# A copy of C taken from SBUF, per-tile first loads and a re-costed planner in a chunked-attention and MLP chain

## The chip, the core and the metric

The kernel runs on one core of one Trainium2 chip. The metric is the device time of one execution in microseconds. Engines are named as in the profile: PE is TensorE, DVE is VectorE, ACT is ScalarE, POOL is GpSimd, SP is SyncE, whose queue issues every DMA here.

## The reference

The inputs are x (4 x 8 x 768 x 32: batch, head, position, width), a (4 x 8 x 768), B and C (4 x 8 x 768 x 16), and four weights. First comes a decaying linear attention, by chunks; then two MLPs on 3072 tokens of width 256 with a hidden width of 2048.

```python
cum = np.cumsum(la, axis=-1)                              # la = log(a) in the chunk
L = np.exp(cum[..., :, None] - cum[..., None, :]) * causal
y[:, :, sl] = einsum('bhij,bhjd->bhid', (Cc @ Bc.T) * L, xc) \
            + einsum('bhin,bhnd->bhid', Cc, state) * np.exp(cum)[..., None]
state = exp(sum(la)) * state + sum_j(Bc x xc * exp(cum[-1] - cum))
...
h = x @ w_in;  g = elu(h);                     x = g @ w_out      # layer 1
h = x @ w_in2; g = h * tanh(softplus(h));      out = g @ w_out2   # layer 2
```

## The kernel before, in words

A chunk has T = 96 positions, so there are 8 chunks; chunk c of batch b is tile i = 4c + b, and the 32 tiles are numbered from 0. The four tiles of a chunk make one block of 384 tokens for the MLPs. The blocks' MLP work is cut into slots (`order`, `at_slot`, L685 to L692): a slot is one group of 128 hidden columns of one layer for one block, so there are 16 slots of layer 1 and 16 of layer 2 for each block, 256 in all. A slot is `emit_h` (L694, six matmuls), the activation on ACT and DVE, from slot 16 on a split of its result into a high and a low part (`split_hi`, `split_lo`, L735 and L741), and `emit_y1` or `emit_y2` (L750, L785). The weights come in 32 jobs of 512 KB (`load_job`, L258) and pass through five steps, `job_1` to `job_5` (L279 to L322), on DVE, ACT and either ACT, DVE or POOL.

A tile of attention loads x (`load_x`, L236), C and B (`load_bc`, L224, and for the four tiles of the first chunk `load_bc0`, L215) and a row of the decays, broadcast over 96 partitions (`at_cumrow`, L453, out of a DRAM copy that `cum_4`, L390, writes). `at_diff`, `at_mask` and `at_exp` make the decay matrix L. For tiles 0 to 2 (`TR0`, L44) C and B are transposed on PE (`at_tr0`, L555), copied out (`at_tr0_out`, L564), and the scores are made in fp32 (`at_scores0`, L587; `at_p0`, L596, multiplies by L). For the other tiles `three_parts` (L893) splits C and B into three bf16 parts: `at_split_1` and `at_split_3` (L459, L470) on ACT, `at_split_2` and `at_split_4` (L465, L476), each of two subtractions, on DVE or POOL, and `at_split_5` (L482), a DMA transpose; `at_scores` and `at_p` follow (L602, L610). From the second chunk on, C is needed a second time, on partitions 96 to 127, three rows of 32 positions beside each other: `load_bc` brings it with three more DMAs from DRAM (L231 to L233). `at_cs` (L523, POOL) scales it, `at_rc` and `at_rc2` (L541, L550) transpose and copy it into the matrix that `at_y` (L627) multiplies by x and the state. `at_y_hi` and `at_y_lo` (L642, L649) take the result out of PSUM as the two parts on which layer 1 works. The transposes, scores and, after the first chunk, the results of a tile share one PSUM buffer, `s`.

The order of all this is set by a planner inside the kernel. Each `step` (L71) names an engine or a choice of engines with a cost in us, a function that issues its instructions, and the steps it depends on. `Ring` (L83) stands for a set of buffers: `take` gives the user of a buffer the list of steps that must be done before it. `run_steps` (L102) first works out for each step how late it may start, then runs a list scheduling with one clock for each engine; SP has a second clock, `moved`, at which the DMA engines are through with what was issued, so a DMA step has the cost of its issue, the time that its data takes, and a landing (L191 to L196). At the end the functions are called in the order of the planned starts, and that is the order of each engine's queue. On the chip each engine takes its queue strictly in order and waits where an input is not there. A cost in the planner therefore never delays anything by itself; it decides what stands in front of what, and on which engine.

```python
late[k] = min([dl] + [late[q] - lat(...) for q in succ[k]]) - sum(...)   # L123
...
k, o, r, cost = min((c for c in can if c[2] <= t + 0.02), key=lambda c: (urgency(c[0], e), c[0]))   # L183
```

Of the kernel before, what the change touches and what calls it, by code (L numbers as in the profile page):

```python
# [17 lines left out]
def tile_chain(  # L18
# [25 lines left out]
    TR0 = (0, 1, 2)  # L44
# [38 lines left out]
    class Ring:  # L83
# [18 lines left out]
    def run_steps():  # L102
# [5 lines left out]
        deps = [sorted(set(flat(e[1]))) for e in steps]  # L108
        succ = [[] for _ in range(n)]
        for k, ds in enumerate(deps):  # L110
            for d in ds:
                succ[d].append(k)
# [6 lines left out]
        while todo:  # L119
# [3 lines left out]
            late[k] = min([dl] + [late[q] - lat(opts[0][0], steps[q][0][0][0]) for q in succ[k]]) - sum(  # L123
                opts[0][3:4], opts[0][1]
            )
            for d in deps[k]:
# [5 lines left out]
        left = [len(deps[k]) for k in range(n)]  # L132
        done = {}
# [12 lines left out]
        def ready(k, e):  # L146
            return max([0.0] + [done[d][1] + lat(done[d][0], e) for d in deps[k]])
# [16 lines left out]
        for _ in range(n):  # L164
            best = None
            for e, ks in open_.items():
                can = []
                for k, o, r, cost in ks:
                    opts = steps[k][0]
                    if len(opts) > 1:  # L170
# [15 lines left out]
            t = max(t, r)  # L186
            free[e] = t + loads(k, e) + cost
# [14 lines left out]
        for _, k, o in sorted(order):  # L202
            steps[k][0][o][2]()
# [11 lines left out]
    def load_bc0(src, d, tag):  # L215

        t = tp.tile([T, NB, H, N], F32, tag=tag, name="bc0")
        nc.sync.dma_start(
            out=t.rearrange("p b h n -> p (b h) n"), in_=src[:, :, 0:T, :].rearrange("b h s n -> s (b h) n")
        )  # L220
        for i in range(NB):
            d[i] = t[:, i]

    def load_bc(i):  # L224
# [600 lines left out]
    s_lc = step((DQ, 0.48, lambda: load_bc0(Cm, c_t, "xyh"), 1.34))  # L825
    s_lb = step((DQ, 0.48, lambda: load_bc0(Bm, b_t, "xyl"), 1.34))
# [7 lines left out]
    s_q4 = [step((DQ, 0.62, lambda c=c: cum_4(c), 0.07), s_q3) for c in range(NCH)]  # L834
# [26 lines left out]
    w_ready = {}  # L861
    r_1, _ = take("raw")
    r_2, _ = take("raw")
    for j, (key, k) in enumerate(jobs):
        rf, rn = take("raw") if j >= NJ else ([], [])
        q0 = step((DQ, 0.48, lambda j=j: load_job(j), 1.46), rn)
        q1 = step((V, 0.42, lambda j=j: job_1(j)), q0)
# [25 lines left out]
    def three_parts(i, need):  # L893
# [23 lines left out]
    for i in range(NB):  # L917
        cold = i in TR0
        if cold:
            tf, tn = take("s")  # L920
            tr = step((PE, 0.64, lambda i=i: at_tr0(i)), s_lc, s_lb, s_c2, tn)
# [4 lines left out]
        else:  # L926
            a2, a5, tf = three_parts(i, [s_lc, s_lb])
# [10 lines left out]
        else:  # L938
# [30 lines left out]
        y = step((PE, 0.95, lambda i=i: at_y(i)), pz, LX[i], an)  # L969
# [5 lines left out]
        bw = step((G, 0.36, lambda i=i: at_bw_1(i)), s_lb, s_d3, bn)  # L975
# [14 lines left out]
    for i in range(NB, tiles):  # L990
        c, b = divmod(i, NB)
        bcf, bcn = take("bc")
        lb = step((DQ, 2.38, lambda i=i: load_bc(i), 0.4), bcn)
# [4 lines left out]
        for g in range(2):  # L998
            f = lambda e, i=i, g=g: at_diff(i, g * H // 2, (g + 1) * H // 2, e)
            dd.append(step(alt(f, (G, 0.79), (V, 0.47)), lc, s_q6))  # L1000
        mk = step((G, 0.85, lambda i=i: at_mask(i)), dd)
        ex = step((A, 0.73, lambda i=i: at_exp(i)), mk)
        table[ex] = "exp"
        cs = step((G, 0.79, lambda i=i: at_cs(i)), lb, lc, s_d5)
        r_f, r_n = take("r")
        rc = step((V, 0.47, lambda i=i: at_rc(i)), cs, r_n)
        rc2 = step(alt(lambda e, i=i: at_rc2(i, e), (V, 0.27), (A, 0.41)), rc)
        bcf += [a2, cs]
        if c + 1 < NCH:
            bf, bn = take("bw")  # L1010
            b1 = step((G, 0.36, lambda i=i: at_bw_1(i)), lb, s_d3, bn)
# [116 lines left out]
```

## Time and profile before

| | us |
|---|---|
| median of the runs shown (3 runs) | 660.62 |
| lowest and highest | 657.75, 661.45 |
| the profiled execution, its own time | 658.91 |
| its span, first to last instruction | 657.2 |
| mean granted clock of PE in it | 0.974 of full speed |

A row of the timeline gives the start, the duration, the engine, the line, the operation, its output and input and how many instructions were merged into it; in brackets stands how long the engine was idle just before, and what ended that. A row by line gives busy us, the mean of one in ns, then idle time in front. A row of waits reads "who waited <- for whom: us in total, times, longest". A DMA row gives KB of each and the median us from issue to landing.

### The profile page before, as it was taken

To read this page: it belongs to the slowest core of one execution; us is meant where nothing else is said; L and a number is where in the kernel's file an instruction comes from. 1 tells how busy PE (TensorE), PEld (TensorE's weight loads), DVE (VectorE), ACT (ScalarE), POOL (GpSimd) and SP (SyncE) were. 2 spreads that over 40 slices of the span, in tenths; PEclk is the share of its full clock that TensorE was granted. 3 is DMA by queue.
4 is the path that set the end of the run, shared out by engine and by line. 5 is a ranking of instruction groups with operands and counts; after the bars stand their busy time and mean duration, and the time that the engine had idled before them with its cause. 6 is when DMAs were issued, how large, how long until landed. Compare 5 with 4: busy or idle time off the path is not lost.

```text
span 657.2 us, 12318 instructions
## 1 busy us (share of the span) xinstructions
PE 613.4 (93%) x4488; PEld 583.4 (89%) x4488; DVE 490.0 (75%) x1018; ACT 370.1 (56%) x704; POOL 190.4 (29%) x220
## 2 busy tenths in 40 slices
PE   4578898999999999999899999999999989999996
PEld 4466668999989989998899989999999989999996
DVE  5699999997579899647975689758985586654443
ACT  4576758696367656445855477445865464442221
POOL 3478584301054484005410244003410040000000
PEclk9569998999999999999999999999999999999999
DMA  8897875331355473015530264105430120000000
GB/s 149 181 280 175 190 150 141 118 113 49 73 91 92 81 117 58 1 10 101 88 58 1 50 99 83 26 0 104 88 58 0 43 43 17 9 1 1 9 18 24
DMA packets 160221, 49.14 MB, mean 75 GB/s; under 512 B 145920, under 2 KB 148992, under 8 KB 160160
## 3 DMA queue, kind: packets, MB, share of 16 engines
q1 hardware_dynamic: 160160, 48.36, 35.5%
q8 instruction: 35, 0.57, 0.4%
q14 instruction: 26, 0.21, 0.1%
HBM read 33.69 MB, written 3.24 MB: 56 GB/s over the span
## 4 chain that ended last, share of the span: by engine, by line
PE 65%; DVE 16%; DMA 10%; issue 3%; SPq 2%; ACT 1%; POOL 1%; DVEq 0%; POOLq 0%; ACTq 0%
PE h L702 10%; PE h L703 10%; PE h L704 10%; DMA d<-cum_d 6%; PE acc L793 6%; PE acc L764 5%; PE acc L765 5%; PE acc L766 5%; PE acc L795 5%; PE acc L794 5%; DVE raw L298 2%; DMA raw<-in_moe_w_in_dram 2%; DMA t<-stk 2%; DVE r L612 2%; DVE gl L744 1%
## 5 line engine op out<-in xcount | busy, mean ns | idle before, releaser
L702 PE MATMUL h<-xyh,wi 128*128 128x384 f32 x512 | 177.6, 347 | 3.0 <-ACT xyh L647 2.9
L703 PE MATMUL h<-xyl,wi 128*128 128x384 f32 x512 | 173.1, 338 | 1.3 <-DVE xyl L653 1.3
L704 PE MATMUL h<-xyh,wi 128*128 128x384 f32 x512 | 172.7, 337 | 0.0
L744 DVE TENSOR_TENSOR gl<-w,gh 128x384 fp32r<-128x384 f32 x221 | 135.8, 614 | 20.4 <-ACT gh L306 8.6
L748 ACT ACTIVATE w<-h 128x384 f32<-128x384 f32 x128 | 61.8, 490 | 106.6 <-PE h L704 104.4
L793 PE MATMUL acc<-wo,gh 128*128 128x256 f32 x384 | 112.7, 293 | 0.2 <-DVE xyl L780 0.2
L795 PE MATMUL acc<-wo,gl 128*128 128x256 f32 x384 | 108.2, 282 | 0.0
L794 PE MATMUL acc<-wo,gh 128*128 128x256 f32 x384 | 108.1, 282 | 0.0
L702 PEld LDWEIGHTS h<-xyh,wi 128*128 128x128 f32 x512 | 97.6, 191 | 5.7 <-ACT xyh L647 3.2
L703 PEld LDWEIGHTS h<-xyl,wi 128*128 128x128 f32 x512 | 97.5, 191 | 2.5 <-DVE xyl L653 2.0
L308 DVE CAST gh<-w 128x384 fp32r<-128x384 f32 x135 | 53.2, 394 | 60.3 <-PE acc L794 38.9
L704 PEld LDWEIGHTS h<-xyh,wi 128*128 128x128 f32 x512 | 97.1, 190 | 0.0
L717 ACT ACTIVATE w<-h 128x384 f32<-128x384 f32 x112 | 54.5, 488 | 49.8 <-PE h L704 49.5
L764 PE MATMUL acc<-gh,wo 128*128 128x384 f32 x224 | 75.6, 338 | 2.7 <-DVE xyl L780 2.7
L766 PE MATMUL acc<-gl,wo 128*128 128x384 f32 x224 | 75.4, 337 | 0.0
L765 PE MATMUL acc<-gh,wo 128*128 128x384 f32 x224 | 75.4, 337 | 0.0
L793 PEld LDWEIGHTS acc<-wo,gh 128*128 128x128 f32 x384 | 72.5, 189 | 2.1 <-DVE xyl L780 0.5
L795 PEld LDWEIGHTS acc<-wo,gl 128*128 128x128 f32 x384 | 72.8, 190 | 0.0
L794 PEld LDWEIGHTS acc<-wo,gh 128*128 128x128 f32 x384 | 72.6, 189 | 0.0
L306 ACT ACTIVATE gh<-w 128x384 fp32r<-128x384 f32 x105 | 55.0, 524 | 29.2 <-PE acc L765 21.6
L725 DVE TENSOR_SCALAR w<-w 128x384 f32<-128x384 f32 x99 | 40.5, 410 | 30.2 <-ACT w L717 29.9
L493 POOL TENSOR_TENSOR d<-d,dk 96x384 f32<-96x384 f32 x35 | 37.4, 1075 | 83.1 <-DMA d<-cum_d 80.2
(103 smaller groups left out, 951.5 us busy)
## 6 DMA issues: line engine op xcount, KB each, us to landing
d<-cum_d SPq DMA_DIRECT2D x31, 288.0 KB, 3.6
raw<-in_moe_w_in_dram SPq DMA_DIRECT2D x16, 512.0 KB, 4.2
raw<-in_moe_w_out_dram SPq DMA_DIRECT2D x16, 512.0 KB, 4.4
xs<-in_x_dram SPq DMA_DIRECT2D x32, 96.0 KB, 3.3
out_dram<-o SPq DMA_DIRECT2D x16, 96.0 KB, 1.9
bc<-in_C_dram SPq DMA_DIRECT2D x28, 48.0 KB, 2.3
bc<-in_B_dram SPq DMA_DIRECT2D x28, 48.0 KB, 2.7
bc<-in_C_dram SPq DMA_DIRECT2D x84, 16.0 KB, 2.1
```

The source lines that it names most:

```text
L306: nc.scalar.activation(out=out, in_=in_, func=AF.Copy)
L702: nc.tensor.matmul(out=h, lhsT=hi[:, k, fs], rhs=xh[:, k, :], start=(k == 0), stop=False)
L703: nc.tensor.matmul(out=h, lhsT=hi[:, k, fs], rhs=xl[:, k, :], start=False, stop=False)
L704: nc.tensor.matmul(out=h, lhsT=lo[:, k, fs], rhs=xh[:, k, :], start=False, stop=(k == 1))
L744: alu(eng).tensor_tensor(out=gl, in0=w, in1=gh.bitcast(F32), op=ALU.subtract)
L748: nc.scalar.activation(out=new_w(s), in_=st[s][0], func=AF.Mish)
L764: nc.tensor.matmul(out=y, lhsT=hi[:, f % FP, ds], rhs=gh, start=(f == 0), stop=False)
L765: nc.tensor.matmul(out=y, lhsT=lo[:, f % FP, ds], rhs=gh, start=False, stop=False)
L766: nc.tensor.matmul(out=y, lhsT=hi[:, f % FP, ds], rhs=gl, start=False, stop=(f == NF - 1))
L793: nc.tensor.matmul(out=y, lhsT=gh[:, ts], rhs=hi[:, f % FP, :], start=(f == 0), stop=False)
L794: nc.tensor.matmul(out=y, lhsT=gh[:, ts], rhs=lo[:, f % FP, :], start=False, stop=False)
L795: nc.tensor.matmul(out=y, lhsT=gl[:, ts], rhs=hi[:, f % FP, :], start=False, stop=(f == NF - 1))
```

## The change

It does five things. `load_bc0` brings one tile of C or B per call, so the first block is loaded by eight DMAs into the same two buffers. `TR0` takes in tile 3, which so goes the way of tiles 0 to 2. The three loads of C for partitions 96 to 127 move out of `load_bc` into a step of their own, `load_c96`, which copies from the tile of C already in SBUF and depends on its landing. The planner gets three rules: the first users of a ring's buffers start in the order of the ring (`Need`, `after`), the steps of a list in `in_turn` start in the order of that list, and POOL's steps and the DVE steps in `lock` are never planned at the same time (`held`). And many costs are changed. Steps that start at the same planned time are now issued in the order in which they were planned. The work is otherwise the same; which engine takes a step that has a choice can differ. Of the diff some cost lines and repeats are left out.

```diff
-    TR0 = (0, 1, 2)
+    TR0 = (0, 1, 2, 3)
...
+    lock = set()
+    in_turn = []
...
-            return self.free[k], (self.free[k - self.n] if k >= self.n else [])
+            return self.free[k], Need(self, k, self.free[k - self.n] if k >= self.n else [])
+    class Need:
+        def __init__(self, ring, k, free):
+            self.ring, self.k, self.free = ring, k, free
...
+        after = [[] for _ in range(n)]
+        for ks in in_turn:
+            for p, q in zip(ks, ks[1:]):
+                after[q].append(p)
+        for users in first.values():
+            ks = [users[q] for q in sorted(users)]
+            for p, q in zip(ks, ks[1:]):
+                if p != q and p not in deps[q]:
+                    after[q].append(p)
         succ = [[] for _ in range(n)]
         for k, ds in enumerate(deps):
-            for d in ds:
+            for d in ds + after[k]:
                 succ[d].append(k)
...
+            late[k] = min([late[k]] + [late[q] for q in succ[k] if k not in deps[q]])
...
-            return max([0.0] + [done[d][1] + lat(done[d][0], e) for d in deps[k]])
+            return max([0.0] + [done[d][1] + lat(done[d][0], e) for d in deps[k]] + [begun[d] for d in after[k]])
...
+                    if e == V and k in lock:
+                        r = max(r, held[G])
+                    elif e == G:
+                        r = max(r, held[V])
...
+            begun[k] = t
+            if e == G or e == V and k in lock:
+                held[e] = t + cost
...
-        for _, k, o in sorted(order):
+        place = {k: i for i, (_, k, _) in enumerate(order)}
+        for _, _, k, o in sorted((t, place[k], k, o) for t, k, o in order):
...
-    def load_bc0(src, d, tag):
-        t = tp.tile([T, NB, H, N], F32, tag=tag, name="bc0")
-        nc.sync.dma_start(
-            out=t.rearrange("p b h n -> p (b h) n"), in_=src[:, :, 0:T, :].rearrange("b h s n -> s (b h) n")
-        )
-        for i in range(NB):
-            d[i] = t[:, i]
+    def load_bc0(src, d, tag, i):
+        if i == 0:
+            tl[tag] = tp.tile([T, NB, H, N], F32, tag=tag, name="bc0")
+        d[i] = tl[tag][:, i]
+        nc.sync.dma_start(out=d[i], in_=src[i, :, 0:T, :].rearrange("h s n -> s h n"))
     def load_bc(i):
...
         sl = slice(c * T, (c + 1) * T)
         nc.sync.dma_start(out=t[0:T, 0], in_=Cm[b, :, sl, :].rearrange("h s n -> s h n"))
         nc.sync.dma_start(out=t[0:T, 1], in_=Bm[b, :, sl, :].rearrange("h s n -> s h n"))
+        c_t[i], b_t[i], c96_t[i] = t[0:T, 0], t[0:T, 1], t[T:128]
+    def load_c96(i):
         for k in range(3):
-            sl = slice(c * T + 32 * k, c * T + 32 * k + 32)
-            nc.sync.dma_start(out=t[T:128, k], in_=Cm[b, :, sl, :].rearrange("h s n -> s h n"))
-        c_t[i], b_t[i], c96_t[i] = t[0:T, 0], t[0:T, 1], t[T:128]
+            nc.sync.dma_start(out=c96_t[i][:, k], in_=c_t[i][32 * k:32 * k + 32])
...
-    s_lc = step((DQ, 0.48, lambda: load_bc0(Cm, c_t, "xyh"), 1.34))
-    s_lb = step((DQ, 0.48, lambda: load_bc0(Bm, b_t, "xyl"), 1.34))
+    s_lc = [step((DQ, 0.48, lambda i=i: load_bc0(Cm, c_t, "xyh", i), 0.95)) for i in range(NB)]
+    s_lb = [step((DQ, 0.48, lambda i=i: load_bc0(Bm, b_t, "xyl", i), 0.95)) for i in range(NB)]
...
-    s_q4 = [step((DQ, 0.62, lambda c=c: cum_4(c), 0.07), s_q3) for c in range(NCH)]
+    s_q4 = [step((DQ, 0.62, lambda c=c: cum_4(c), 0.2), s_q3) for c in range(NCH)]
...
-        q1 = step((V, 0.42, lambda j=j: job_1(j)), q0)
+        q1 = step((V, 0.36, lambda j=j: job_1(j)), q0)
+        lock.add(q1)
...
+        lock.add(q3)
+        q4 = step(alt(lambda e, j=j: job_4(j, e), (A, 0.58), (V, 0.34)), q3)
+        q5 = step(alt(lambda e, j=j: job_5(j, e), (G, 1.33), (V, 0.60)), q4,
                   dl=slot_time(2 * NF + k * FP) + 10.0 if j >= NJ else 1e9)
+        lock.update((q4, q5))
...
-        LX[i] = step((DQ, 0.48, lambda i=i: load_x(i), 0.55), n)
+        LX[i] = step((DQ, 0.48, lambda i=i: load_x(i), 0.95), n)
+    in_turn.append([s_la])
+    for i in range(NB):
+        in_turn[-1] += [s_lc[i], s_lb[i], LX[i]] + LW[i:i + 1]
...
-        a2 = step(alt(lambda e: at_split_2(i, e), (V, 0.40), (G, 0.78)), a1, rn)
+        a2 = step(alt(lambda e: at_split_2(i, e), (V, 0.40), (G, 0.45)), a1, rn)
         a3 = step((A, 0.62, lambda: at_split_3(i)), a2)
-        a4 = step(alt(lambda e: at_split_4(i, e), (V, 0.40), (G, 0.78)), a3)
+        a4 = step(alt(lambda e: at_split_4(i, e), (V, 0.40), (G, 0.45)), a3)
         tf, tn = take("t")
-        a5 = step((DQ, 0.62, lambda: at_split_5(i), 1.34, True), a4, tn)
+        a5 = step((DQ, 0.62, lambda: at_split_5(i), 2.0, True), a4, tn)
+        lock.update((a2, a4))
...
-            sc = step((PE, 0.33 if cold else 0.24, lambda z=z: at_scores(i, z)), a5, pn)
+            sc = step((PE, 0.4 if cold else 0.33, lambda z=z: at_scores(i, z)), a5, pn)
...
-            tr = step((PE, 0.64, lambda i=i: at_tr0(i)), s_lc, s_lb, s_c2, tn)
+            tr = step((PE, 0.64, lambda i=i: at_tr0(i)), s_lc[i], s_lb[i], s_c2, tn)
...
-                dd.append(step(alt(f, (G, 0.79), (V, 0.47)), lc, s_q6))
-        mk = step((G, 0.85, lambda i=i: at_mask(i)), dd)
-        ex = step((A, 0.73, lambda i=i: at_exp(i)), mk)
+                dd.append(step(alt(f, (G, 1.0), (V, 0.47)), lc, s_q6))
+                lock.add(dd[-1])
+        mk = step((G, 0.95, lambda i=i: at_mask(i)), dd)
+        ex = step((A, 0.78, lambda i=i: at_exp(i)), mk)
...
-                sc = step((PE, 1.3, lambda i=i, z=z: at_scores0(i, z)), cp, hn, an)
+                sc = step((PE, 0.7, lambda i=i, z=z: at_scores0(i, z)), cp, hn, an)
                 gf.append(sc)
-                pz.append(step((V, 0.54, lambda i=i, z=z: at_p0(i, z)), sc, ex, r_n))
+                pz.append(step((V, 0.61, lambda i=i, z=z: at_p0(i, z)), sc, ex, r_n))
...
-        lb = step((DQ, 2.38, lambda i=i: load_bc(i), 0.4), bcn)
+        lb = step((DQ, 0.96, lambda i=i: load_bc(i), 1.9), bcn)
+        l96 = step((DQ, 1.44, lambda i=i: load_c96(i), 0.15), lb)
...
-        cs = step((G, 0.79, lambda i=i: at_cs(i)), lb, lc, s_d5)
+        cs = step((G, 0.95, lambda i=i: at_cs(i)), l96, lc, s_d5)
         r_f, r_n = take("r")
-        rc = step((V, 0.47, lambda i=i: at_rc(i)), cs, r_n)
+        rc = step((V, 0.56, lambda i=i: at_rc(i)), cs, r_n)
         rc2 = step(alt(lambda e, i=i: at_rc2(i, e), (V, 0.27), (A, 0.41)), rc)
+        lock.add(rc2)
...
-        h = HS[s] = step((PE, 1.95 if s < 2 else 0.98, lambda s=s: emit_h(s)), src, w_ready[f"i{layer}", f // FP], hn,
+        h = HS[s] = step((PE, 1.95 if s < 2 else 1.04, lambda s=s: emit_h(s)), src, w_ready[f"i{layer}", f // FP], hn,
...
-            two = [(G, 0.96), (V, 0.47)]
+            two = [(G, 1.01), (V, 0.47)]
...
-            y = YS[s] = step((PE, 0.98 if split else 1.29, lambda s=s: emit_y1(s)), ydep, an, YS.get(s - 1, []), dl=ydl)
+            y = YS[s] = step((PE, 1.04 if split else 1.29, lambda s=s: emit_y1(s)), ydep, an, YS.get(s - 1, []), dl=ydl)
...
-                y = step((PE, 0.326, lambda s=s, k=k: emit_y2(s, k)), ydep, an[k] if an else [], prev, dl=ydl)
+                y = step((PE, 0.355, lambda s=s, k=k: emit_y2(s, k)), ydep, an[k] if an else [], prev, dl=ydl)
```

## Rows read from the trace of the kernel before

**Rows 1.** Page, part 1: engine, busy us (share of the span), instructions.

```profile
PE 613.4 (93%) x4488; PEld 583.4 (89%) x4488; DVE 490.0 (75%) x1018; ACT 370.1 (56%) x704; POOL 190.4 (29%) x220
```

**Rows 2.** Busy us of PE, PEld, DVE, ACT, POOL by stretch; PEclk, DMA, GB/s.

```profile
0.00:40.00 40.00, 20.68 (x189) 16.50 (x190) 26.95 (x65) 20.44 (x41) 16.55 (x26) 0.70 0.88 189
40.00:104.00 64.00, 54.99 (x345) 41.71 (x344) 62.91 (x112) 43.27 (x89) 48.17 (x49) 0.98 0.78 181
104.00:630.00 526.00, 516.29 (x3797) 504.01 (x3798) 390.41 (x823) 301.65 (x566) 125.69 (x145) 1.00 0.28 56
630.00:657.20 27.20, 21.39 (x160) 21.19 (x158) 9.70 (x22) 4.70 (x10) 0.00 (x0) 0.94 0.06 16
```

**Rows 3.** Timeline: start us, us, instruction [idle <-releaser]; last, ScalarE waits, 0 to 104.

```profile
23.56 0.48 ACT L306 ACTIVATE f32t<-p_tr 112x384 f32<-112x384 f32 x1
...
29.74 0.71 PE L634 MATMUL ys<-r,xs 96*32 96x96 f32 x12
...
30.50 0.31 ACT L647 ACTIVATE xyh<-ys 128x192 fp32r<-128x192 f32 x1
32.92 0.70 ACT L291 ACTIVATE raw<-raw 128x512 f32<-128x512 f32 x1 [2.11 <-DMA raw<-in_moe_w_in_dram]
...
34.14 0.30 ACT L647 ACTIVATE xyh<-ys 128x192 fp32r<-128x192 f32 x1
...
35.31 0.69 PE L702 MATMUL h<-xyh,wi 128*128 128x384 f32 x1 [2.93 <-ACT xyh L647]
37.28 0.69 PE L703 MATMUL h<-xyl,wi 128*128 128x384 f32 x1 [1.28 <-DVE xyl L653]
...
ACT raw L291 <- DMA raw<-in_moe_w_in_dram: 6.8, 5, 2.1
```

**Rows 4.** Chain of waits, 27 to 33 us: start us, us, what.

```profile
27.14 5.77 DMA raw<-in_moe_w_in_dram
```

**Rows 5.** DMA, 0 to 10 us (packets, MB, share); 10 to 20; after 105.

```profile
q1 hardware_dynamic: 8778, 1.28, 82.3%
...
bc<-in_C_dram SPq DMA_DIRECT2D x1, 192.0 KB, 3.7
bc<-in_B_dram SPq DMA_DIRECT2D x1, 192.0 KB, 5.2
...
bc<-in_C_dram SPq DMA_DIRECT2D x2, 48.0 KB, 5.3
...
bc<-in_C_dram SPq DMA_DIRECT2D x20, 48.0 KB, 2.1
```

**Rows 6.** Timeline of SP; then tile bc: ns min/median/max, first and last.

```profile
1.82 2.19 SPq L218 DMA_DIRECT2D bc<-in_B_dram  x1
...
12.57 3.11 SPq L233 DMA_DIRECT2D bc<-in_C_dram  x3
...
L233 SPq DMA_DIRECT2D bc<-in_C_dram x84: 448/452/2099, 12.6 to 477.5; - x84
...
L526 POOL TENSOR_TENSOR d<-bc,dk x28: 865/934/1481, 31.2 to 533.8; 32x384 f32<-32x384 f32 x28
```

**Rows 7.** Timeline of VectorE: start us, us, instruction.

```profile
10.75 1.17 DVE L480 TENSOR_TENSOR stk<-r,stk 96x128 bf16<-96x128 f32 x2
```

**Rows 8.** VectorE by line, 40 to 104 us, then after; last, its timeline.

```profile
L298 DVE SCALAR_TENSOR_TENSOR raw<-raw 128x512 int32<-128x512 int32 x15 | 13.2, 885 | 0.0
...
L725 DVE TENSOR_SCALAR g<-g 128x384 f32<-128x384 f32 x10 | 6.7, 673 | 0.1
...
L725 DVE TENSOR_SCALAR w<-w 128x384 f32<-128x384 f32 x96 | 39.1, 409 | 30.2 <-ACT w L717 29.9
...
12.88 0.68 DVE L298 SCALAR_TENSOR_TENSOR raw<-raw 128x512 int32<-128x512 int32 x1
```

**Rows 9.** Waits of TensorE, 104 to 657 us: us in total, times, longest.

```profile
PE ys L634 <- DVE r L612: 5.8, 10, 1.2
```

**Rows 10.** Line 468 on POOL: ns min/median/max, first and last start.

```profile
L468 POOL TENSOR_TENSOR r<-bc,stk x16: 424/530/1234, 20.9 to 408.7; 96x128 f32<-96x128 f32 x16
```

More of the change, by code (lines that the diff above doesn't have):

```diff
@@ L108, in run_steps, with needs @@
         deps = [sorted(set(flat(e[1]))) for e in steps]
+        first = {}
+        def needs(k, d):
+            if isinstance(d, Need):
+                first.setdefault(d.ring, {}).setdefault(d.k, k)
+            elif isinstance(d, (list, tuple)):
+                for e in d:
+                    needs(k, e)
+        for k, e in enumerate(steps):
+            needs(k, e[1])
+        after = [[] for _ in range(n)]
[7 more added lines that the diff above has]
+                    after[q].append(p)
         succ = [[] for _ in range(n)]
         for k, ds in enumerate(deps):
-            for d in ds:
+            for d in ds + after[k]:
                 succ[d].append(k)
@@ L122, in run_steps @@
             opts, _, dl = steps[k]
-            late[k] = min([dl] + [late[q] - lat(opts[0][0], steps[q][0][0][0]) for q in succ[k]]) - sum(
-                opts[0][3:4], opts[0][1]
-            )
-            for d in deps[k]:
+            late[k] = min([dl] + [late[q] - lat(opts[0][0], steps[q][0][0][0]) for q in succ[k] if k in deps[q]])
+            late[k] -= sum(opts[0][3:4], opts[0][1])
+            late[k] = min([late[k]] + [late[q] for q in succ[k] if k not in deps[q]])
+            for d in deps[k] + after[k]:
                 left[d] -= 1
@@ L130, in run_steps @@
         assert seen == n, "a cycle of steps"
-        left = [len(deps[k]) for k in range(n)]
-        done = {}
+        left = [len(deps[k]) + len(after[k]) for k in range(n)]
+        done, begun = {}, {}
+        held = {V: 0.0, G: 0.0}
         open_ = {e: [] for e in (DQ, A, V, G, PE)}
@@ L858, in tile_chain @@
     af.append(s_d7)
-    w_ready = {}
+    w_ready, LW = {}, []
     r_1, _ = take("raw")
@@ L870, in tile_chain @@
         q3 = step((V, 0.65, lambda j=j: job_3(j)), q1, q2)
-        q4 = step(alt(lambda e, j=j: job_4(j, e), (A, 0.52), (V, 0.34)), q3)
-        q5 = step(alt(lambda e, j=j: job_5(j, e), (G, 1.23), (V, 0.60)), q4,
+        lock.add(q3)
+        q4 = step(alt(lambda e, j=j: job_4(j, e), (A, 0.58), (V, 0.34)), q3)
+        q5 = step(alt(lambda e, j=j: job_5(j, e), (G, 1.33), (V, 0.60)), q4,
                   dl=slot_time(2 * NF + k * FP) + 10.0 if j >= NJ else 1e9)
+        lock.update((q4, q5))
         rf.append(q5)
         w_ready[key, k] = [q4, q5]
+        LW.append(q0)
         if key == "o1":
@@ L926, in tile_chain @@
         else:
-            a2, a5, tf = three_parts(i, [s_lc, s_lb])
+            a2, a5, tf = three_parts(i, [s_lc[i], s_lb[i]])
             bc0_f.append(a2)
@@ L968, in tile_chain @@
         af, an = take("acc")
-        y = step((PE, 0.95, lambda i=i: at_y(i)), pz, LX[i], an)
+        y = step((PE, 0.8, lambda i=i: at_y(i)), pz, LX[i], an)
         r_f.append(y)
@@ L974, in tile_chain @@
         bf, bn = take("bw")
-        bw = step((G, 0.36, lambda i=i: at_bw_1(i)), s_lb, s_d3, bn)
+        bw = step((G, 0.42, lambda i=i: at_bw_1(i)), s_lb[i], s_d3, bn)
         bc0_f.append(bw)
@@ L999, in tile_chain @@
             f = lambda e, i=i, g=g: at_diff(i, g * H // 2, (g + 1) * H // 2, e)
-            dd.append(step(alt(f, (G, 0.79), (V, 0.47)), lc, s_q6))
-        mk = step((G, 0.85, lambda i=i: at_mask(i)), dd)
-        ex = step((A, 0.73, lambda i=i: at_exp(i)), mk)
+            dd.append(step(alt(f, (G, 1.0), (V, 0.47)), lc, s_q6))
+            lock.add(dd[-1])
+        mk = step((G, 0.95, lambda i=i: at_mask(i)), dd)
+        ex = step((A, 0.78, lambda i=i: at_exp(i)), mk)
         table[ex] = "exp"
-        cs = step((G, 0.79, lambda i=i: at_cs(i)), lb, lc, s_d5)
+        cs = step((G, 0.95, lambda i=i: at_cs(i)), l96, lc, s_d5)
         r_f, r_n = take("r")
-        rc = step((V, 0.47, lambda i=i: at_rc(i)), cs, r_n)
+        rc = step((V, 0.56, lambda i=i: at_rc(i)), cs, r_n)
         rc2 = step(alt(lambda e, i=i: at_rc2(i, e), (V, 0.27), (A, 0.41)), rc)
+        lock.add(rc2)
         bcf += [a2, cs]
@@ L1010, in tile_chain @@
             bf, bn = take("bw")
-            b1 = step((G, 0.36, lambda i=i: at_bw_1(i)), lb, s_d3, bn)
-            b2 = step((G, 0.36, lambda i=i: at_bw_2(i)), s_d7, b1)
+            b1 = step((G, 0.42, lambda i=i: at_bw_1(i)), lb, s_d3, bn)
+            b2 = step((G, 0.42, lambda i=i: at_bw_2(i)), s_d7, b1)
             bcf.append(b1)
@@ L1051, in tile_chain @@
             e = step(alt(lambda e, s=s: elu_2(s, e), (V, 0.27), (A, 0.41)), e)
+            lock.add(e)
             e = step((V, 0.47, lambda s=s: elu_3(s)), e)
@@ L1062, in tile_chain @@
             gh = step(alt(lambda e, s=s: split_hi(s, e), *(two if layer == 1 else two[::-1])), e, gn)
-            two = [(G, 0.96), (V, 0.47)]
+            two = [(G, 1.01), (V, 0.47)]
             gl = step(alt(lambda e, s=s: split_lo(s, e), *(two if layer == 1 else two[::-1])), gh, ln)
+            lock.update((gh, gl))
             wf.append(gl)
```

3 lines of the change are left out of this document (2 added, 1 removed).

## The prediction

> **What bounds the kernel now.** I read the page first, then the busy time of the engines by stretch. TensorE is busy for 93% of the span [rows 1], but that average hides two regimes. From 104 to 630 us it is busy for 516.3 of 526 us, and 9.7 us are lost; the last 27.2 us lose 5.8 more. Before 104 us VectorE sets the pace: from 40 to 104 us it is busy for 62.9 of 64 us, while TensorE gets 55.0. In the first 40 us neither is full: TensorE 20.7 us, VectorE 27.0, and the DMA engines have a mean share of 0.88 [rows 2]. So time can come from three places: up to 13 us of idle VectorE before 40 us, VectorE's work up to 104 us, and the 9.7 us of stalls behind it. The 516 us of matmuls stay, because no layer matmul is touched.
>
> The timeline around the first layer matmul shows what goes wrong in the start. That matmul stands at 35.31 us and its partner, which needs the low halves, at 37.28. The attention outputs of the first block were all in PSUM by 29.74 + 0.71 = 30.45 us, and ScalarE took one of them out at 30.50. Then ScalarE, which runs in order, sat 2.11 us for a weight that landed at 32.9, and the next eviction came only at 34.14 [rows 3]. The order was written for a weight that arrives earlier: the planner charges 1.46 us of DMA time for each, and the chain of waits holds a landing of 5.77 us [rows 4].
>
> **The loads of the first block.** Two transfers of 192 KB become eight of 48 KB, and `in_turn` forces the order a, then C, B, x and one weight for each tile. The bytes are the same. The old loads landed after 3.7 and 5.2 us, and the issue of B alone held SP for 2.19 us [rows 5, 6]; eight issues at the median 0.45 us of L233 [rows 6] make 3.6 us, where the old B alone takes 2.19. Small packets are what these loads cost: in the first 10 us 8778 packets kept 16 engines 82.3% busy [rows 5], which is 131.7 / 8778 = 15 ns each, so the 1536 packets of one tile's C and B take 1536 x 15 / 16 = 1.4 us. Tile 0 could then start some 2 us earlier, but x and C and B of tile 3 come behind three weights. At the 1.28 MB of the first 10 us (128 GB/s) and the 189 of the first 40 [rows 2, 5], the 3.3 MB up to there (0.9 of a, C, B and x, 1.5 of weights, 0.9 of decay rows) take 17 to 26 us. From the first landing at 2 to 3 us, tile 3 is complete between 20 and 29 us; then it needs transposes, a copy, scores, products, y and evictions, about 7 us, as tile 2 took 6.9 from ScalarE's copy at 23.56 to the last product at 30.45 [rows 3]. The layer could start between 27 and 36 us, where it now stands at 37.3. I take 31: if only ScalarE's false wait goes, 37.3 becomes about 33 (34.14 minus 30.81, the end of the eviction before, is 3.3 us of it), and the other waits of ScalarE for weights in the start (6.8 us in five waits, this one among them [rows 3]) are worth some 2 more. That is 6 us earlier.
>
> The Trainium skill ("DMA: Bandwidth & Descriptors", Rules for kernel authors) says to coalesce many small transfers, since under 64 KB one pays mostly overhead; 48 KB is under that. By it the split loses: this is the second rival's case, and the issue times above price it.
>
> How much of 6 us reaches the end? VectorE has a fixed amount to do up to the point where TensorE takes over, so the gain is the part of its 13 idle us that disappears. A shift of the layer by 6 us fills most of a like amount; I take 5 us, with bounds 0 and 9.
>
> **Tile 3 without the split.** It drops a pair of subtractions in each of two steps, four ScalarE copies and a DMA transpose; two products become four of half the width. One of the pairs took VectorE 1.17 us [rows 7], so some 1 to 2 us of VectorE go, less a copy of PSUM if that falls to it, in a stretch where it idles: I count it inside the 5 us. TensorE takes 4 more transposes and trades 8 score matmuls for 8 others, at a mean granted clock of 0.70; it is half idle there [rows 2]. Tile 3 now stands in the queue for the one PSUM buffer `s`, as tiles 0 to 2 do, and for ScalarE's copy: that is in the 7 us.
>
> **The second copy of C.** 84 transfers of 256 packets of 64 B become 84 of 32 packets of 512 B. At 15 ns over 16 engines, 768 packets cost 0.72 us of all DMA engines per tile, 20 us over the run, but only the two tiles loaded before 45 us (1.4 us) fall where DMA is full. Three of them held SP for 3.11 us at 12.57, against 3 x 0.45 when quiet [rows 6]. The price is a new wait: the copy reads what the C load wrote, so SP, in order, stands until that has landed, 2.1 us after its issue when quiet and 5.3 in the start [rows 5]. Behind it on SP stand a transpose, a decay row or a weight. The planner now charges 0.96 + 0.65 + 1.9 = 3.5 us before it issues the copy, which covers the quiet landing and leaves up to 2 us of SP waiting in the start. The consumer at tile 4, POOL's product, starts at 31.2 us [rows 6], 10 us after 12.57 + 3.11 + 5.3, so a copy that is 2 to 3 us later is covered. I take 0, bounds -1.4 and +2.
>
> **The recalibrated planner.** Nothing is computed anew; the order of the instructions and the choice of engine change. Two corrections matter. First, `lock` makes POOL and certain VectorE steps exclude each other in the plan. The trace shows why: between 40 and 104 us the weight step of L298 takes 885 ns, where one at 12.88 us took 0.68, and L725 takes 673, against 409 later [rows 8]. That is 15 x 0.20 + 10 x 0.26 = 5.6 us in these two forms alone that VectorE spends on nothing, with POOL busy for 48.2 of these 64 us [rows 2]. If plan and chip agree on when POOL works, part of it goes, but the POOL work must still be done: I take a third, -2, bounds -6 and +4. Second, slots of TensorE are charged 1.04 us for 0.98 and the attention steps nearer to their traces. After 104 us the waits of y for L612 make 5.8 of 9.7 us [rows 9]; I take -1, bounds -4 and +5.
>
> **Sum.** -5 - 2 - 1 = -8 us on the profiled execution, whose span is 657.2 and whose own time is 658.91 us (1.71 around the span), 1.7 under the median of 660.62 of the runs shown. That gives 651 us.
>
> **Rivals.** *Hidden (0.20).* An earlier layer only moves the wait, because VectorE is full from 40 us on: the idle time of the start stays in another place, and the planner trades one stall for another. Then -1 to +1 is left: 658 us, in 656 to 662. For it: 62.9 of 64 us [rows 2]. Against it: VectorE's own 13 idle us before. *Small transfers cost (0.05).* The six extra issues and the three weights ahead of tile 3 hold the layer at 36 to 39 us; the issues add 6 x 0.4 = 2.4 us to the profiled 658.9, so 658 to 661.5, say 660. The overhead that the Trainium skill names would act so; the trace has the 48 KB loads land in 2.1 us when quiet and the 192 KB ones in 3.7 and 5.2 [rows 5], which speaks against it. *Slower: POOL's splits are underpriced (0.16).* The planner now charges POOL 0.45 us for `at_split_2` and `at_split_4`, each of which is two instructions; the shortest on POOL takes 424 ns and the median one 530 [rows 10], so a pair is 0.85 to 1.06. Every tile that goes there has its transposed copy about 0.4 to 0.6 us late per step, 0.8 to 1.2 in all, while VectorE is blocked as well. It decides where that exceeds the slack before the scores on TensorE. With 24 tiles, half of them stalled by 1 us, the steady part loses 12 us, and with the 5 us of the start regained the time is 666 (662 to 672). Against it: POOL had only 16 of the first kind at the old charge [rows 10], and VectorE, at 0.40, is still tried first. *Larger gain (0.11).* The blocked 5.6 us go too, and the layer starts at 28: -9 - 6 - 2 = -17, 642 us.
>
> **How the numbers follow.** The forecast has 0.48, own range 645 to 656. About 0.5% (3.3 us) is what a measurement of this kernel can tell from no change: faster is under 657.3 by the median, slower over 663.9. The forecast and the larger gain give 0.59, and 0.05 of the hidden case lies under 657.3: 0.64. The rest of the hidden case and the small transfers give 0.20 with the edge of the slower one, and 0.16 is left for slower. The range takes in the forecast, the hidden case and half of the larger gain: 641 to 662.
>
> **What would show it.** Right: the first layer matmul and its partner at 28 to 34 us, no wait of ScalarE for a weight in front of an eviction, VectorE over 29.5 busy us in the first 40 on the old work, L725 and L298 nearer to 409 and 680 ns, and the point at which TensorE is full some 6 to 8 us before 104. Copies of C with 84 issues under 0.5 us. Wrong: the layer at 36 us or later, more idle TensorE than 9.7 us in its full stretch, tiles' splits on POOL in large number with waits of the scores for the transposed copy, or SP standing on the C landing with a weight behind it.

## The result, and the profile after

The kernel after takes 639.95 us (median) against 659.18: a ratio of 0.9716 (interval 0.9662 to 0.9770). The forecast was 651 us, in 641 to 662: the direction was right, the size was not. The profiled execution has a span of 638.9 us, 18.3 under the 657.2 of before. One execution of the run e12 below took 752.65 us, at a granted clock of 0.747, and its ratio is taken without it.

Page, part 1, and busy time by stretch of the kernel after (columns as in [rows 2]: PE, PEld, DVE, ACT, POOL, then granted clock, DMA share, GB/s):

```profile
PE 614.3 (96%) x4500; PEld 584.1 (91%) x4500; DVE 457.3 (72%) x937; ACT 402.7 (63%) x753; POOL 194.6 (30%) x259
```

```profile
0.00:40.00 40.00, 30.98 (x245) 23.07 (x246) 26.50 (x69) 23.74 (x48) 14.89 (x26) 0.79 0.77 174
40.00:104.00 64.00, 57.38 (x364) 46.72 (x364) 56.88 (x103) 53.08 (x111) 40.21 (x46) 0.97 0.77 184
104.00:630.00 526.00, 522.03 (x3865) 510.60 (x3864) 372.02 (x763) 325.12 (x594) 139.50 (x187) 1.00 0.28 56
630.00:638.90 8.90, 3.87 (x33) 3.66 (x31) 1.90 (x4) 0.77 (x2) 0.00 (x0) 0.97 0.16 44
```

Against [rows 1, 2], VectorE fell from 490.0 to 457.3 us while ScalarE rose from 370.1 to 402.7. Not all of that is work that went from one to the other. ScalarE's 33 us hold twelve more loads of its activation table (44 before, 56 after, 1283 ns each, 15.4 us in all). Here is the costliest group of them, before and after:

```profile
L748 ACT ACT_TABLE_LOAD x22 | 28.2, 1283 | 0.4
...
L791 ACT ACT_TABLE_LOAD x28 | 35.9, 1283 | 0.5
```

Of what left VectorE, a part went to POOL, as the groups further below show. VectorE is no longer full between 40 and 104 us (56.9 of 64, was 62.9).

To see where TensorE's idle time went, one cuts behind 40 us differently. First before, then after:

```profile
40.00:180.00 140.00, 130.53 (x845) 116.42 (x845) 126.72 (x239) 95.17 (x174) 63.44 (x63) 0.98 0.54 136
180.00:630.00 450.00, 440.75 (x3299) 429.30 (x3297) 326.60 (x696) 249.75 (x480) 110.42 (x131) 1.00 0.27 49
```

```profile
40.00:180.00 140.00, 130.66 (x883) 118.28 (x883) 118.77 (x220) 122.51 (x217) 71.66 (x83) 0.98 0.62 150
180.00:630.00 450.00, 448.75 (x3346) 439.04 (x3345) 310.14 (x646) 255.69 (x488) 108.05 (x150) 1.00 0.24 45
```

Idle TensorE, before and after: 19.3 and 9.0 us up to 40 us; 9.5 and 9.3 up to 180; 9.3 and 1.3 up to 630; 5.8 and 5.0 in the rest. That is 43.9 against 24.6, 19.2 us less, with 0.9 us more busy time: the 18.3 us. So by the time axis 10 us were won in the start and 8 in the long, full stretch. The waits of TensorE behind 104 us agree with the second part. The products of tiles (`at_p`, now L655) still head the list, with 3.4 us in two rows; [rows 9] had 5.8 us in 10 waits of the second kind:

```profile
PE s L649 <- DVE r L655: 1.9, 3, 1.3
PE ys L677 <- DVE r L655: 1.5, 2, 0.8
```

The start of the kernel after, in the timeline (ScalarE, then TensorE) and ScalarE's waits for weights up to 104 us; it answers to [rows 3]:

```profile
22.26 0.33 ACT L690 ACTIVATE xyh<-ys 128x192 fp32r<-128x192 f32 x1 [0.41 <-PE ys L677]
...
25.25 0.80 ACT L517 ACTIVATE stk<-r 96x256 bf16<-96x256 f32 x2 [1.83 <-POOL r L511]
25.95 0.64 ACT L334 ACTIVATE raw<-raw 128x512 f32<-128x512 f32 x1
26.50 0.31 ACT L690 ACTIVATE xyh<-ys 128x192 fp32r<-128x192 f32 x1
...
26.86 0.69 PE L745 MATMUL h<-xyh,wi 128*128 128x384 f32 x1 [1.68 <-ACT xyh L690]
27.64 0.69 PE L746 MATMUL h<-xyl,wi 128*128 128x384 f32 x1
...
ACT raw L334 <- DMA raw<-in_moe_w_in_dram: 5.9, 6, 2.1
```

The layer starts at 26.9 and 27.6 us, where it stood at 35.3 and 37.3. ScalarE still waits 5.9 us in all for weights, but none of these waits delays an eviction of the first block now. In front of the last one stands another wait, of 1.83 us for a split of attention on POOL (L511), and TensorE idles 1.68 us for that eviction. TensorE's granted clock rises earlier too: it is 0.50 (1.2 GHz) in the 5 us before each of the two stretches below, in which TensorE was busy for 3.41 and 3.22 us, and 1.00 (2.4 GHz) in the 5 us after each. First the kernel before, then the kernel after:

```profile
40.00:45.00 5.00, 5.00 (x26) 4.47 (x26) 4.97 (x8) 4.31 (x9) 3.90 (x4) 0.70 0.89 311
```

```profile
30.00:35.00 5.00, 5.00 (x31) 3.56 (x30) 3.19 (x7) 2.51 (x6) 2.26 (x4) 0.93 0.98 294
```

### The profile page after: what moved, and what is told of

Read it like the earlier page. It is cut to its first block, busy times and chain, and to the rows that moved or that the text cites. A ratio compares the mean times of both kernels' runs of the same rounds, so it can differ in the third digit from the quotient of the medians.

```text
span 638.9 us, 12337 instructions
## 1 busy us (share of the span) xinstructions
PE 614.3 (96%) x4500; PEld 584.1 (91%) x4500; DVE 457.3 (72%) x937; ACT 402.7 (63%) x753; POOL 194.6 (30%) x259
## 3 DMA queue, kind: packets, MB, share of 16 engines
q1 hardware_dynamic: 139872, 47.96, 35.3%
## 4 chain that ended last, share of the span: by engine, by line
PE 80%; DVE 7%; ACT 4%; DMA 2%; issue 2%; POOL 0%; DVEq 0%; POOLq 0%; ACTq 0%
PE h L745 13%; PE h L746 12%; PE h L747 12%; PE acc L836 7%; PE acc L838 7%; PE acc L837 7%; PE acc L807 5%; PE acc L809 5%; PE acc L808 5%; PE acc L812 3%; PE ys L709 2%; PE ys L677 2%; PE s L649 1%; DMA d<-cum_d 1%; DVE raw L341 1%
## 5 line engine op out<-in xcount | busy, mean ns | idle before, releaser
L787 DVE TENSOR_TENSOR gl<-w,gh 128x384 fp32r<-128x384 f32 x219 | 132.6, 609 | 17.9 <-ACT gh L349 9.0
L351 DVE CAST gh<-w 128x384 fp32r<-128x384 f32 x119 | 50.5, 426 | 59.5 <-PE acc L837 40.0
L349 ACT ACTIVATE gh<-w 128x384 fp32r<-128x384 f32 x121 | 63.3, 523 | 31.1 <-PE acc L808 23.2
L768 DVE TENSOR_SCALAR w<-w 128x384 f32<-128x384 f32 x85 | 33.2, 392 | 40.2 <-ACT w L760 40.0
L536 POOL TENSOR_TENSOR d<-d,dk 96x384 f32<-96x384 f32 x39 | 35.9, 930 | 71.5 <-DMA d<-cum_d 60.5
```

The costliest lines, as they stand in the source:

```text
L349: nc.scalar.activation(out=out, in_=in_, func=AF.Copy)
L787: alu(eng).tensor_tensor(out=gl, in0=w, in1=gh.bitcast(F32), op=ALU.subtract)
```

## The experiments

Each is told with its time and its ratio to the kernel before, measured beside it. The kernel after is 0.9716. "First layer matmul" is its start in us.

**How much is scatter of the planner.** Almost any edit of the planner replans everything, so one control has the due times shifted by 1 us (`return 26.0 + 1.7 * s`).

> Control for the planner's own scatter: the kernel after with all due times of the slots 1 us later, which stands for no physical change. All theories: 640 us; what it is off by is the size of a difference that no single plan should be explained by. I expect up to 4 us.

639.19 us, 0.9693 (0.9646 to 0.9740). Together with the second control, e9 below, differences under some 3 us between single plans are not explained here.

**Costs, rules, copy, first loads.** e1 puts all costs back (of the slots, for example, `(PE, 0.98`, and of the DMAs `load_x(i), 0.55`, `at_split_5(i), 1.34`).

> The kernel after with all of the planner's costs as before (engines and DMA), and its rules, first loads, tile 3 and SBUF copy kept. Theory 1, the corrected costs make most of the gain: 652 to 660 us, and TensorE stalls after 104 us come back to 8 to 12 us. Theory 2, the first loads and their forced order make it: 640 to 645 us, with the first layer matmul still at 26 to 28 us. Theory 3, the rules lock and ring order make it: 640 to 645 us as well, with VectorE below 58 busy us between 40 and 104 us.

e2 takes out the two rules:

```diff
-                    if e == V and k in lock:
-                        r = max(r, held[G])
-                    elif e == G:
-                        r = max(r, held[V])
...
-        for users in first.values():
+        for users in ():
```

> The kernel after without the lock rule and without the ring-order rule in the planner; in_turn, costs, loads kept. Theory 3 (the rules make the gain behind the start): 648 to 656 us, the first layer matmul still at 26 to 28 us, VectorE back above 61 of 64 us between 40 and 104. Theories 1 and 2: 638 to 644 us.

e3 keeps the plan and changes the source of the second copy alone:

```diff
-            nc.sync.dma_start(out=c96_t[i][:, k], in_=c_t[i][32 * k:32 * k + 32])
+            sl = slice(c * T + 32 * k, c * T + 32 * k + 32)
+            nc.sync.dma_start(out=c96_t[i][:, k], in_=Cm[b, :, sl, :].rearrange("h s n -> s h n"))
```

> The kernel after, its plan unchanged instruction by instruction, but load_c96 reads C from DRAM in pieces of 64 B as before instead of from SBUF. What is measured is the SBUF copy by itself. If it is worth nothing, as the prediction has it: 639 to 642 us. If the freed DMA time (0.72 us a tile) carries part of the start: 643 to 648 us, the first layer matmul 1 to 3 us later.

e4 keeps of the change only `load_bc0` by tiles and `in_turn` (the second copy stays a step of its own, but from DRAM).

> Of the change only the first loads tile by tile with the forced order in_turn (tile 3 by the split, old costs, no lock, no ring order, second copy of C from DRAM). Theory 2: the first layer matmul at 27 to 31 us and 648 to 652 us. Theories 1 and 3: 655 to 662 us.

| | us | ratio (interval) | first layer matmul |
|---|---|---|---|
| e1, old costs | 646.68 | 0.9811 (0.9757 to 0.9865) | 40.3 |
| e2, no rules | 657.94 | 0.9986 (0.9961 to 1.0012) | 27.6 |
| e3, copy from DRAM | 638.57 | 0.9694 (0.9635 to 0.9752) | 26.3 |
| e4, first loads alone | 658.65 | 1.0000 (0.9971 to 1.0028) | 36.4 |

e2 is the surprise: with the layer starting as early as in the kernel after, the whole gain is gone. That is outside even the 648 to 656 us expected of theory 3. The start is worth nothing without the rules. e1 is the counterpart, and met none of the three theories: with the rules but the old costs the layer starts at 40.3 us, 5 later than before the change, and the time is still 12 us shorter. e4: the forced order without the costs does not even start the layer earlier. e3: the SBUF copy is worth nothing that shows by itself. The wait that it adds is real, as SP's waits of the kernel after and its issues show (min/median/max ns). Below them stand the issues of e3, then the DMA queue of the kernel after and of e3 (packets, MB, share of 16 engines):

```profile
SPq L277 <- DMA bc<-in_C_dram: 21.8, 14, 2.7
...
L277 SPq DMA_DIRECT2D bc<-bc x84: 513/582/1563, 23.1 to 464.1; - x84
```

```profile
L279 SPq DMA_DIRECT2D bc<-in_C_dram x84: 424/450/2095, 24.4 to 460.2; - x84
```

```profile
q1 hardware_dynamic: 139872, 47.96, 35.3%
...
q1 hardware_dynamic: 158688, 47.96, 36.0%
```

SP stood 21.8 us in 14 waits for the C load to land (28 tiles have such a copy), and one issue of the copy holds SP for 582 ns (median) against 450. e3 has no such wait and moves 18816 packets more. But the 16 DMA engines were busy for 36.0% of 635.2 us with them and for 35.3% of 638.9 us without, 228.7 and 225.5 us: the copy frees some 3 us, not the 20 of the prediction. The two kernels are not told apart.

**Rules and costs apart.** e5 drops the lock rule alone, e6 the ring order alone, e7 takes the old costs for DMAs alone, e8 for the engines alone.

> The kernel after without the lock rule alone (ring order kept). If lock carries what the rules gave (18 us between the kernel after and the one without both): 652 to 660 us, with the stalls of TensorE from 180 to 630 us back near 10 us. If the ring order carries it: 638 to 644 us.

> The kernel after without the ring-order rule alone (lock kept). If the ring order carries it: 652 to 660 us. If lock does: 638 to 644 us. If each carries half: about 648 us here and there.

> The kernel after with the DMA costs of before and all else kept. If the DMA costs made the early start (26.9 us against 40.3 with all costs old): first layer matmul at 36 to 41 us and 645 to 650 us. If the costs of the engines made it: 26 to 29 us and 638 to 642 us.

> The kernel after with the costs of the engines of before and all else kept. If the DMA costs made the early start: first layer matmul at 26 to 29 us and 638 to 643 us. If the engine costs made it: 36 to 41 us and 645 to 650 us.

| | us | ratio (interval) | first layer matmul |
|---|---|---|---|
| e5, no lock | 653.23 | 0.9919 (0.9888 to 0.9950) | 25.4 |
| e6, no ring order | 642.04 | 0.9747 (0.9721 to 0.9773) | 27.2 |
| e7, old DMA costs | 647.10 | 0.9815 (0.9773 to 0.9857) | 34.4 |
| e8, old engine costs | 639.36 | 0.9711 (0.9672 to 0.9751) | 29.7 |

The lock rule carries 13 us (0.9919 less 0.9716 of 659). The ring order is not resolved beside the lock rule (e6); where the lock rule is out, e2 against e5, it gives some 4 us, hardly over the scatter. The early start comes from the DMA costs: in e7 the layer waits as it did before, and 6 to 7 us are lost. Its trace (ScalarE, VectorE, TensorE) has waits for DMAs in front of ready work again:

```profile
29.46 0.68 ACT L334 ACTIVATE raw<-raw 128x512 f32<-128x512 f32 x1 [4.26 <-DMA raw<-in_moe_w_in_dram]
...
30.59 0.30 ACT L690 ACTIVATE xyh<-ys 128x192 fp32r<-128x192 f32 x1
...
27.94 0.55 DVE L536 TENSOR_TENSOR d<-d,dk 96x384 f32<-96x384 f32 x1 [2.30 <-DMA d<-cum_d]
28.41 3.32 DVE L325 TENSOR_SCALAR raw<-raw 128x512 int32<-128x512 int32 x2
31.66 0.68 DVE L341 SCALAR_TENSOR_TENSOR raw<-raw 128x512 int32<-128x512 int32 x1
32.26 1.14 DVE L643 TENSOR_TENSOR r<-s,d 96x192 f32<-96x192 f32 x4
...
25.56 0.99 PE L637 MATMUL s<-f32t 16*96 16x96 f32 x16
...
34.41 0.69 PE L745 MATMUL h<-xyh,wi 128*128 128x384 f32 x1 [0.43 <-ACT xyh L690]
```

ScalarE stands 4.26 us for a weight before it takes out an attention result (30.59). The scores of tile 3 are there at 26.55 us, but VectorE's products of them (L643) come only at 32.26, behind a wait for a decay row and three weight steps. The charge of a weight's own load is 1.46 us in both kernels, so the difference can only come by the charges of the other transfers, which the plan's clock `moved` adds up. Which of the five did it was not tried.

The engine costs, the many small corrections, are worth nothing that shows. In e8 the layer even starts 2.8 us later than in the kernel after, at no loss of time.

**How the lock rule works.** The planner's pass is run twice: the first picks the engine of each step, the second plans the order with these fixed. e9 has the rule in both passes, e10 in the first alone, e11 in the second alone.

```diff
+        fix = {k: o for _, k, o in plan(True, None)}      # e11: plan(False, None)
+        order = plan(False, fix)                          # e9, e11: plan(True, fix)
```

> Control for the next two: the kernel after, planned twice with the lock rule, the second pass keeping the engine that the first chose for each step. Both theories: 637 to 644 us.

> The engines chosen by a pass with the lock rule, the order planned by a second pass without it. If the rule works by moving steps from VectorE to ScalarE: 638 to 645 us. If it works by putting POOL beside the VectorE steps that it does not block: 650 to 656 us.

> The engines chosen by a pass without the lock rule, the order planned by a second pass with it. If the rule works by moving steps from VectorE to ScalarE: 649 to 657 us, ScalarE near 94 busy us between 40 and 180. If by the order: 638 to 645 us.

e9: 642.55 us, 0.9746 (0.9699 to 0.9793). e10: 644.78, 0.9789 (0.9751 to 0.9828). e11: 654.13, 0.9920 (0.9896 to 0.9945). The choice of engines carries the larger part of the rule: e10 has it alone and gains 8 to 9 of the 13 us against e5. The order alone (e11) gains nothing, and on top of the choice it gives 2 us (e9) to 5 (the kernel after), which is hardly over the scatter. Between 40 and 180 us it is the choice that relieves VectorE. Here are e10, then e11 with its full stretch:

```profile
40.00:180.00 140.00, 128.98 (x852) 115.66 (x851) 119.52 (x209) 109.47 (x202) 63.11 (x73) 0.95 0.55 142
...
40.00:180.00 140.00, 123.62 (x796) 109.33 (x796) 127.11 (x245) 99.34 (x173) 60.98 (x65) 0.94 0.56 143
180.00:630.00 450.00, 447.51 (x3333) 437.16 (x3332) 325.18 (x701) 254.23 (x480) 87.97 (x121) 1.00 0.26 47
```

In e11 TensorE loses only 2.5 us between 180 and 630 us, so the order does remove stalls there; but it loses 16.4 before, with VectorE at 127.1 of 140, and the time is no better. What moved is seen in the groups by line, first before, then after (busy us, mean ns, idle in front):

```profile
L306 ACT ACTIVATE gh<-w 128x384 fp32r<-128x384 f32 x105 | 55.0, 524 | 29.2 <-PE acc L765 21.6 <-PE acc L794 4.5 <-DVE w L733 1.8
...
L723 ACT ACTIVATE w<-w 128x384 f32<-128x384 f32 x13 | 6.8, 525 | 0.3
...
L480 POOL TENSOR_TENSOR stk<-r,stk 96x128 bf16<-96x128 f32 x10 | 5.6, 583 | 6.5 <-ACT stk L474 6.5
L723 ACT ACTIVATE g<-g 128x384 f32<-128x384 f32 x6 | 3.1, 522 | 0.2
```

```profile
L349 ACT ACTIVATE gh<-w 128x384 fp32r<-128x384 f32 x121 | 63.3, 523 | 31.1 <-PE acc L808 23.2 <-PE acc L837 6.8 <-DVE w L768 0.4
...
L523 POOL TENSOR_TENSOR stk<-r,stk 96x128 bf16<-96x128 f32 x36 | 18.5, 533 | 34.1 <-ACT stk L517 34.0
L511 POOL TENSOR_TENSOR r<-bc,stk 96x128 f32<-96x128 f32 x32 | 18.1, 583 | 17.3 <-ACT stk L506 8.6 <-DVE g L776 5.5 <-DMA bc<-in_B_dram 2.6
L766 ACT ACTIVATE w<-w 128x384 f32<-128x384 f32 x27 | 14.1, 521 | 0.6
L766 ACT ACTIVATE g<-g 128x384 f32<-128x384 f32 x15 | 7.5, 522 | 0.2
```

42 layer-1 slots instead of 19 have `elu_2` on ScalarE, and 121 high splits instead of 105; of the attention splits, 68 instructions instead of 26 are on POOL ([rows 10] for the first kind). Not all of this is the lock rule, since POOL's charge for these splits fell too, from 0.78 to 0.45 us. The kernel after without the rule (e5) has 26, 98 and 40 of the three; the kernel before with nothing but the rule (e13, below) has 43, 117 and 40. So `elu_2` and the high splits went with the rule, and the attention splits by the lower charge and the rule. By the code, a locked VectorE step may not start before POOL is done, so VectorE's clock in the plan runs later; `end()`, which compares the options, reads that clock, so the other option ends sooner there and the planner takes it.

e17 takes only the slots' engines from the locked pass, e18 only those of all other steps; both are ordered without the rule, as e10.

> Order planned without the lock rule, as in e10; the engines of the MLP slots' steps (elu_2, high and low split) taken from a pass with the lock rule, those of all other steps from a pass without it. If the steps of the slots that go from VectorE to ScalarE and POOL carry the gain (e10 644.8 against e5 653.2): 644 to 648 us. If the weight and attention steps carry it: 650 to 654 us.

> The other way round: slots' engines from the pass without the lock rule, weights' and attention's from the pass with it. If the slots' steps carry the gain: 650 to 654 us. If the splits and differences of attention that go to POOL carry it: 644 to 648 us. If both are needed: 648 to 651 us here and in e17.

e17: 649.67 us, 0.9843 (0.9787 to 0.9899). e18: 647.11, 0.9798 (0.9731 to 0.9865). Both lie between e5 and e10. Only the half of weights and attention (e18) is clear of e5; the interval of the slots' half (e17) touches that of e5, and the two halves are not told apart.

**The rule alone, and other ways to the same end.** e13 adds the rule to the kernel before, with nothing else. e14 takes it out of the kernel after and charges VectorE its measured times instead (`elu_2` 0.40, high split 0.42, low split 0.61, `job_3` 0.83 and so on; ScalarE's options 0.52); e15 has both.

> The kernel before with the lock rule alone; costs, loads, tile 3, ring order as before. If the lock rule is the main part and stands by itself: 645 to 650 us, stalls of TensorE from 180 to 630 us under 4 us, first layer matmul still after 34 us. If it needs the ring order or the new costs beside it: 653 to 660 us.

> The kernel after without the lock rule, but with VectorE's steps charged what the profile shows them to take, blocked time included (elu_2 0.40 for 0.27, the high split 0.42 for 0.27, the low split 0.61 for 0.47, job_3 0.83 for 0.65 and so on), and ScalarE's alternatives at 0.52 for 0.41. If what matters is that the planner sees how full VectorE is and moves steps off it: 639 to 646 us, ScalarE above 110 busy us between 40 and 180. If the exclusion of POOL itself is needed: 650 to 656 us.

> The same charges with the lock rule kept. If a fuller VectorE in the plan only helps up to the point where TensorE is fed: 637 to 643 us, no better than the kernel after. If more steps off VectorE still help: 630 to 637 us. The blocked time is then counted twice, so it can also overshoot: over 645.

e13: 646.34 us, 0.9789 (0.9742 to 0.9835), with the layer still at 37.5 us. Its full stretch:

```profile
180.00:630.00 450.00, 447.70 (x3337) 438.34 (x3336) 308.37 (x653) 253.39 (x496) 111.23 (x141) 1.00 0.26 47
```

TensorE loses 2.3 us there, 9.3 before. e5, the kernel after without the rule, loses 6.6 (near 10 was expected), and up to 180 us another 11.8, with VectorE at 126.8 of 140 and a granted clock of 0.94 against 0.98 in the kernel after. Over the whole execution some 8 of its 12 us more are idle time of TensorE, and 4 are busy time of TensorE, 618.4 us for 614.3:

```profile
40.00:180.00 140.00, 128.22 (x818) 114.63 (x817) 126.81 (x244) 93.85 (x170) 59.09 (x59) 0.94 0.53 137
180.00:630.00 450.00, 443.40 (x3320) 432.35 (x3319) 331.09 (x699) 251.75 (x476) 92.73 (x127) 1.00 0.26 49
```

e14: 648.87 us, 0.9828 (0.9782 to 0.9875), about half of the rule's worth and in neither expected range; VectorE is still busy for 127.0 of the 140 us between 40 and 180. e15: 646.39, 0.9784 (0.9730 to 0.9838), 6 us more than the kernel after, though the intervals overlap and though VectorE has the least to do of all:

```profile
40.00:180.00 140.00, 125.83 (x821) 112.11 (x820) 111.79 (x199) 114.89 (x214) 73.52 (x74) 0.95 0.57 143
```

VectorE is busy for 111.8 of 140 us there and TensorE idles for 14.2, where the kernel after has 118.8 and 9.3. So relief of VectorE does not by itself make a plan faster. Which steps have to leave it was not shown. The theory that the true prices do the same as the rule has fallen.

**The tile-by-tile loads.** e16 keeps the plan; the first call of `load_bc0` brings all four tiles.

> The kernel after, its plan unchanged, but the first of the four calls of load_bc0 brings all four tiles (192 KB) and the other three bring nothing. What is measured is the tile-by-tile load by itself. If it carries the start: first layer matmul 2 us or more later and 642 to 645 us. If it is worth nothing: 638 to 642 us.

644.04 us, 0.9752 (0.9697 to 0.9808); the layer starts at 29.3 us, 2.4 later than after. The time is 4 us more, but the intervals overlap, so a gain in time from the split loads is not shown; in e8 a start as late (29.7 us) cost nothing. Undoing `in_turn` alone or tile 3 alone was not tried.

## Why the prediction was wrong

**The lock rule was mis-sized, through the wrong mechanism.** The step said -2 us, a third of the 5.6 us that VectorE spends blocked, because "the POOL work must still be done". It asked what the rule does to collisions, and not what it does to `end()`, which picks the engine. The collisions on the steps that stayed hardly changed. The weight step of L298, 885 ns in [rows 8], stands first here, from the kernel after between 40 and 104 us; then come the `elu_2` steps left on VectorE in that stretch:

```profile
L341 DVE SCALAR_TENSOR_TENSOR raw<-raw 128x512 int32<-128x512 int32 x15 | 11.9, 797 | 0.1
...
L768 DVE TENSOR_SCALAR w<-w 128x384 f32<-128x384 f32 x2 | 0.9, 430 | 0.0
```

The first is 15 x 0.09 = 1.3 us. The blocked time of the second form, 2.6 of the 5.6 us, is gone because the steps are: 2 in place of 13. The rule is worth 13 us (e5) or 14 (e13), for the larger part by steps that leave VectorE (e10, e11).

**The steady stalls.** The step gave -1 us to slots charged 1.04 us and to better attention costs. Measured: 8 us less idle between 180 and 630 us, and nothing from the engine costs (e8). The lock rule is the main cause: it takes 7 of 9.3 us in the kernel before (e13) and 5 of the 6.6 of e5. Its choice (e10, 2.1 us left) and its order (e11, 2.5) each do that by themselves. The ring order has a part in it too: without it (e6) 5.8 us are idle there, though the time is 2 us more only.

**The start was right in kind and too small.** I took the layer at 31 us, 6 us before the partner's 37.3, with 5 reaching the end; the partner starts at 27.6 and the first matmul at 26.9, at the early edge of the 27 to 36. (37.3 less the 3.3 us of the false wait is 34, not the "about 33" of the working.) The false wait of ScalarE was the right thing to read, but I put its removal under the first loads and their order. The runs put it under the DMA costs (e7, 7.5 us of start); the loads and their order alone give nothing (e4), and with the new costs the loads by tiles give 2.4 us of start (e16). The step also took the gain to be the part of VectorE's 13 idle us that disappears, since "VectorE has a fixed amount to do". That premise failed: VectorE is busy for 26.5 of the first 40 us, where it was 27.0 and over 29.5 was the sign. TensorE idles 10 us less there all the same, and the amount of VectorE's work is what the change did alter. That the start reaches the end only if VectorE can keep up was in the hidden rival, and e2 is that rival: layer at 27.6 us, 657.94 us. The rules are what kept it from deciding.

**The copy of C at nothing** was right in time (e3), with the predicted wait on SP in place. The 20 us of DMA time in that step were not: 3 us were measured, and the issues are over 0.5 us each. **Tile 3** at nothing was not tried alone.

**The rivals.** POOL's underpriced splits came as described, 68 on POOL for 26, 40 of them without the lock rule (e5). No wait of TensorE's scores for the transposed copy followed behind 40 us; what it cost is the 1.83 us of ScalarE in front of the first block's last eviction. The small transfers showed no cost; the Trainium skill's rule on coalescing ("DMA: Bandwidth & Descriptors", Rules for kernel authors) would have these 48 KB loads lose, and e16 shows the 192 KB ones slower to the layer, 29.3 against 26.9 us. The larger gain, 642 us, came nearest in number, and its early layer came (28, measured 26.9); its blocked time did not go from the weight steps, and the lock rule's choice of engines was no part of it.

## What to carry to other kernels

A planner's cost or rule has to be followed into every decision that reads it: here the exclusion of POOL and VectorE was worth 13 us, 8 to 9 of them through the choice between engines alone, and nothing through the order alone. Where an engine is 98% busy in a stretch, ask first what lets work leave it; an earlier start only pays once it can (e2 against the kernel after). Here correcting the costs of transfers paid (e7) and correcting those of instructions did not (e8): in e7 one step on ScalarE, planned for a weight that came later, held up a ready eviction behind it for 4.26 us.

## What was not expected of the hardware

Cutting the second copy from 64 B to 512 B pieces took away 18816 packets, but only some 3 us of all DMA engines, where the packets of the first 10 us had promised some 20 (15 ns each); neither that nor 21.8 us of SP standing still moved the time by anything that shows (e3, 638.57 us). ScalarE was busy for 33 us more, 15 of them in loads of its table, its share going from 56% to 63%, while TensorE's idle time fell by 19 us.
